# Hashed attention and top-1 experts on one core: block transpositions behind the first product, and six steps moved between pairs

## The chip, the core and the metric

One NeuronCore of a Trainium2 chip runs the whole program. The metric is device microseconds of one execution; a kernel's time is the median of its runs.

## What is computed

Bucketed attention over 4 batches of 8 heads, 768 tokens of 64 elements, then a mixture of 8 experts in which each of the 3072 tokens goes to one:

```python
q_bits = (np.einsum('bhsd,dk->bhsk', q, proj) > 0)      # 6 bits; k_bits the same way
mask = q_bucket[:, :, :, None] == k_bucket[:, :, None, :]
scores = np.where(mask, scale * np.matmul(q, k.transpose(0, 1, 3, 2)), -1e9)
attn = np.exp(scores - scores.max(-1)); attn /= attn.sum(-1) + 1e-09
x = np.matmul(attn, v)                                  # to (3072, 512)
expert_idx = np.argmax(x @ w_gate, axis=1)
for e in range(8):
    y[expert_idx == e] = np.maximum(x[expert_idx == e] @ w1[e], 0.0) @ w2[e]
return gate_w[:, None] * y
```

## The kernel before

**Attention part (0 to some 460 us).** Heads are worked off in 16 pairs (g = 0 to 15, four to a batch). A pair has twelve units of 128 query rows (six for each head). Unit i goes through S (score, four matrix products, L306 and L308), R (row maximum on VectorE, DVE, L316), A (its factor, L321 to L325, on DVE or GpSimd, POOL), X (exponential on ScalarE, ACT, L332), which frees the score's buffer in PSUM, of which there are three. The first six units are then transposed on TensorE (PE) (T, L346) and copied out (E, L370 or L372); the last six are transposed in blocks on DVE (D, L386), and the next pair sends them to `pt` with 16 transfers (L396): Y0, three of four block rows, twelve transfers, and Y1, the last four. V and B are the products with the values (L407), of which B10 is the first that uses exchanged `pt`. O, K, L and M bring the result to token rows `xr` (L412, L426, L436, L416).

For the next pair, G and H compute the hash bits (L261, L241), w scales them on ACT and writes them to DRAM (`lsh_bits`, L274 and L275), and z reads them into the operands as mask rows (`mask`, L279, on POOL's queue). C are POOL's casts and subtractions of the next pair's q and k (`part`, L205 to L213).

Once a batch (four pairs) is done, its tokens are routed in the second pair that follows (`route`, steps Z0 to Z6 in pairs 5, 9 and 13) and their rows are scattered to `sorted_rows`, six scatters a batch (`scatter`, steps N0 to N3, L498 to L501, on POOL). In a pair the N steps come in the order N2 (early), N0 (middle), N3 and N1 (end). `sorted_rows` is first filled with empty rows, eight fills, one an expert (`fill`, L147), issued from `before`.

The order of all this is written by hand: the strings HEAD, NEXT, PLAN and LAST list the steps of pair 0, 1, 2 to 14 and 15, and every engine, and the DMA queue of SyncE (SP), executes its share in this order. A "-" behind a step means the pair before.

From the first three batches' counts `pick_first` chooses the expert to begin with, in four pieces: the keys (L518 to L521), their maximum (L528, L530), the index (L534 to L536), and its load into SP's register (L539), after which the first raw weights are loaded.

**Expert part.** Nine phases of a first product (`mm1`, eight column groups f, L774), ReLU in two parts (`relu`: high on ACT, L788, low on DVE, L790) and a second product (`mm2`, L811, or by token in `yout`, L831). Phases 0 and 1 are 256 tokens each of the first expert, phases 2 to 8 one expert each, of 456 down to 354 tokens. While phase n runs, the rows of n+1 are read (`rows`, `xg`), transposed in blocks on DVE (`blocks`, L722, four or three of them), and split into high and low parts (`xt`: ACT L741, DVE L742). The raw weights of the next expert are split on ACT and POOL (`halves`, L679, L680). In phases 3 to 5 small steps of a plan for spilled tokens run on DVE between them (L572 to L635).

Of the kernel before, what the change touches and what calls it, by code (L numbers as in the profile page):

```python
# [53 lines left out]
def lsh_attention_moe(ctx, tc, qk2, v, proj, wg, w1, w1q, w2, out):  # L54
# [17 lines left out]
    def load_x(h):  # L72
        g = h // 2
        if g == NG - 1:
            x = (wk if h % 2 else moe).tile([128, 2 * S], F32, name="xl" if h % 2 else "xhe", bufs=1)
        else:
            x = room[:, h % 2] if g % 2 else wk.tile([128, 2 * S], F32, name="xd")
        for c in ((S, 2 * S), (0, S)) if h < 2 else ((0, 2 * S),):
            nc.sync.dma_start(x[:, c[0]:c[1]], qk2[h][:, c[0]:c[1]])
        XD[h] = x  # L80

    def load_v(g):
        VT[g] = wk.tile([128, NT, 2, D], F32, name="vt")
        nc.sync.dma_start(VT[g], v[g])
# [409 lines left out]
    def scatter(b, hf, ts=(0, 1, 2)):  # L494
        slot, x = SL[b, hf], XR[b, hf]
        t0 = b * NT + hf * 3
        if ts[0] == 0:
            nc.gpsimd.tensor_copy(x[:, :, GC + 1].bitcast(I32), C["tokid"][:, t0:t0 + 3])  # L498
        for t in ts:
            nc.gpsimd.memset(C["spacer"], 0.0)  # L500
            st = nc.gpsimd.indirect_dma_start(  # L501
                out=xs, out_offset=bass.IndirectOffsetOnAxis(ap=slot[:, t:t + 1], axis=0),
                in_=x[:, t], in_offset=None)
            for o in scat:
                tc.declare_no_dep(st.ins, o.ins, reason="slots of other tokens")
            scat.append(st)
# [9 lines left out]
    def keys(name):  # L516
        k = const.tile([128, E], F32, name=name)
        nc.vector.tensor_tensor(k, C["base"], C["base0"], op=OP.subtract)  # L518
        C["cnt"] = const.tile([128, E], F32, name=name + "_c")
        nc.vector.tensor_copy(C["cnt"], k)  # L520
        nc.vector.scalar_tensor_tensor(k, k, float(E), C["desc"], op0=OP.mult, op1=OP.add)  # L521
        return k

    def pick_first():
        k = keys("key0")
        yield
        t = const.tile([128, 4], F32, name="pf")
# [255 lines left out]
    M1 = {}  # L783
# [8 lines left out]
    def by_token(n):  # L792
        return PH[n][2] <= 384
# [87 lines left out]
        nc.sync.dma_start(wgt[:, :, s * (PW - E):s * (PW - E) + E], wg[:, :, s * E:(s + 1) * E])  # L881
    NC = NU // 2
    FREE = ("00v", "10v")
    routes, parts, pick = {}, list(range(16)), pick_first()

    def weights(n):
# [8 lines left out]
    def weight_half(op, x):  # L895
# [30 lines left out]

    NEXT = """
        S0 E40a- R0 L0- S1 X11- S2 T41- E41a- C00 C01 C02 A0V T42- E42a- X0 T50- E50a- T51- E51a- T52- E52v- G R1 A1P
        R2 S3 H A2V X1 R3 X2 V1- T00 C03 E00v A3P C04 S4 O1- M1- T01 S5 X3 R4 E01a C05 A4V R5 A5V T02 T10 w X4 E02a
        C06 E10v S6 R6 X5 A6V S7 C10 C11 T11 E11a T12 S8 E12v K1- L1- T20 X6 R7 T21 S9 E20a E21a A7P z0 R8 A8P C12 X7  # L930
        T22 R9 A9P X8 E22a D6 S10 D7 S11 C13 D8 X9 B00 R10 C14 z1 A10P R11 A11P B01 C15 D9 X10 X11 C16 D10 D11 M0 M1
    """.split()

    PLAN = """
        Y0- S0 R0 O0- S1 S2 C00 C01 C02 A0V X0 G R1 A1P R2 S3 H A2V X1 R3 K0- X2 L0- T00 C03 E00v A3P C04 S4 Z0 T01 S5
        X3 R4 E01a C05 A4V Z1 R5 A5V T02 T10 w Y1- X4 N2 E02a C06 E10v S6 R6 X5 A6V S7 Z2 C10 Z3 Z4 C11 T11 E11a Z5
        T12 S8 E12v T20 X6 R7 T21 S9 Z6 E20a N0 E21a A7P z0 R8 A8P C12 X7 T22 R9 A9P X8 E22a B10- D6 S10 D7 S11 C13 D8
        B11- X9 B00 R10 C14 z1 A10P R11 A11P B01 C15 D9 X10 X11 N3 O1- C16 K1- N1 D10 D11 M0 M1 L1-
    """.split()

    LAST = """
        Y0- S0 O0- R0 K0- S1 L0- X0 Y1- R1 S2 S3 R2 X1 X2 S4 T00 T01 R3 E00a E01a R4 S5 X3 R5 T02 X4 X5 E02v T10 S6
        E10a T11 T12 E11a R6 S7 T20 S8 R7 E12a T21 X6 S9 E20v X7 E21v B10- B11- O1- M0 R8 T22 E22a x0 R9 X8 T30 X9 g0
        V0 E30a x2 h0 O0 T31 S10 g2 E31a T40 T32 h2 R10 E40a S11 T41 R11 E32a K0 E41v nA m0 L0 r0 X10 T42 X11 nA E42a
        T50 M1 tP E50a r0 m1 T51 nA r0 T52 E51a m2 E52a tP tV u0 u1 nP r0 tP u2 r0 r0 nA V1 d0 nP r0 O1 tP d1 K1- K1
# [13 lines left out]
    def scatter_step(g, k):  # L959

        b, q = divmod(g - NP, NP)
        if 0 <= b < B - 1:
            at = {(q, k): 2 * q + k - 2 for q in (1, 2, 3) for k in (0, 1)}
            if b == B - 2:
                at |= {(2, 2): 2, (2, 0): 3, (2, 3): 4, (2, 1): 5}
            if (q, k) in at:
                scatter(b, at[q, k] // 3, (at[q, k] % 3,))

    def before(c):

        g, r = divmod(c, 6)
        if r == 3 and g + 2 < NG:
            load_x(2 * g + 4)
            load_x(2 * g + 5)
        if g + 1 < NG and r == (5 if g else 4):
            load_v(g + 1)
        if g < 2 and r > 3:
            fill(4 * g + 2 * r - 8)
            fill(4 * g + 2 * r - 7)

    def behind(i):

# [10 lines left out]
    def step(g, w):  # L993
# [7 lines left out]
        if op == "S":  # L1001
            i = 12 * n + int(x)
            if i % 2 == 0:
                before(i // 2)
# [26 lines left out]
        elif op == "E":  # L1031
            trans_ev(6 * n + int(x[0]), int(x[1]), x[2] == "v" and not (n % NP == 1 and n > NP and x in FREE))
        elif op == "V":
# [45 lines left out]
    last = [route(B - 1, (0,)), route(B - 1, (1,))]  # L1079
    for g in range(NG):  # L1080
        for w in {0: HEAD, 1: NEXT, NG - 1: LAST}.get(g, PLAN):
            step(g, w)
            if g == NG - 2 and w in ("R5", "R7", "R9", "S11"):
                next(pick, None)
                if w == "S11":
                    raw_load(0, 0)
                    raw_load(0, 1)
            if g == NG - 1 and w == "R9":
                GT[0] = moe.tile([128, 4], F32, name="gate", bufs=3)
                nc.vector.tensor_copy(GT[0][:, :2], XG[0][:, :, GC])  # L1090
                tokens(0)
# [18 lines left out]
    def halves(n, k):  # L1110

        if n < 4 * E:
            chunk_part(n + k // 4, k % 4)
            if k % 2:
                h = 2 * n + k // 2 + 3
                if h < LASTH:
                    raw_load(h // 2, h % 2)


    WHEN = (((0,), (1,)), ((2,), (3,)), ((), ()), ((), ()))  # L1120
    raw_load(5, 0)
    plan = spill_plan()
    for n in range(1, len(PH)):
        c0 = 4 * (PH[n][0] + 1)
        last = n + 1 == len(PH)
        if not last:
            rows(n + 1)
        for f in range(8):
            mm1(n, f)
            if f % 2 and not by_token(n - 1):  # L1130
                yout(n - 1, f // 2)
            halves(c0, f)
            if not last and f > 3:
                blocks(n + 1, f - 4)
            if 3 <= n < 6:
                for _ in range(2):
                    next(plan, None)
        for m in range(4):
            mid, end = ((), ()) if last else WHEN[m]
            if not (last and m == 3):  # L1140
                mm2(n, m, lambda: xts(n + 1, mid))
            halves(c0 + 2, 2 * m)
            halves(c0 + 2, 2 * m + 1)
            xts(n + 1, end)
        if n == 6:
# [69 lines left out]
```

## Time and profile before

| | |
|---|---|
| median of 3 runs | 763.74 us (760.83 to 765.19) |
| profiled execution | 767.85 us |
| its span, first to last instruction | 766.1 us |
| PE busy | 718.8 us, 94% |
| DVE, ACT, POOL busy | 489.8, 413.8, 487.2 us |
| mean granted clock of PE | 0.977 |

The times are those of one core, so the span is nearly the whole time. A busy PE is not a PE at its peak, since matrix products are pipelined, but an idle one is lost time. A wait in square brackets behind a row is the idle time of that engine just before it, with what is taken to have ended it; where an instruction waits for several things, only the last by the profile is named.

### The profile page before, as it was taken

To read this page: it belongs to the slowest core of one execution; us is meant where nothing else is said; L and a number is where in the kernel's file an instruction comes from. 1 tells how busy PE (TensorE), PEld (TensorE's weight loads), DVE (VectorE), ACT (ScalarE), POOL (GpSimd) and SP (SyncE) were. 2 spreads that over 40 slices of the span, in tenths; PEclk is the share of its full clock that TensorE was granted. 3 is DMA by queue.
4 is the path that set the end of the run, shared out by engine and by line. 5 is a ranking of instruction groups with operands and counts; after the bars stand their busy time and mean duration, and the time that the engine had idled before them with its cause. 6 is when DMAs were issued, how large, how long until landed. Compare 5 with 4: busy or idle time off the path is not lost.

```text
span 766.1 us, 13486 instructions
## 1 busy us (share of the span) xinstructions
PE 718.8 (94%) x4575; PEld 577.4 (75%) x4575; DVE 489.8 (64%) x936; ACT 413.8 (54%) x836; POOL 487.2 (64%) x729
## 2 busy tenths in 40 slices
PE   8997899999989999999988999699999999999996
PEld 3765676667757766676566788589989899989895
DVE  6757888889879888998797672324573825242321
ACT  5765766677658666776566632434334344453310
POOL 8635656677767687866766563384656666668532
PEclk7999999999999999999999999899999999999999
DMA  5949776768787768786649336664737386737301
GB/s 188 297 135 327 212 194 177 206 187 216 200 222 203 219 159 221 222 237 157 195 130 247 125 133 189 174 164 159 179 104 181 136 127 180 188 130 197 113 10 37
DMA packets 69928, 135.58 MB, mean 177 GB/s; under 512 B 15572, under 2 KB 32212, under 8 KB 69857
## 3 DMA queue, kind: packets, MB, share of 16 engines
q1 hardware_dynamic: 63024, 118.31, 56.4%
q0 software_dynamic: 6688, 16.35, 6.4%
q8 instruction: 37, 0.61, 0.4%
q14 instruction: 35, 0.28, 0.1%
q10 hardware_dynamic: 144, 0.03, 0.0%
HBM read 75.79 MB, written 26.33 MB: 133 GB/s over the span
## 4 chain that ended last, share of the span: by engine, by line
PE 65%; DVE 11%; issue 7%; ACT 7%; POOL 5%; DMA 4%; SPq 1%; POOLq 0%; DVEq 0%; ACTq 0%; another core or an unknown queue 0%
PE s L774 14%; PE t L407 14%; PE s L811 10%; PE s L831 8%; PE s L306 6%; DVE m L316 5%; ACT e L332 5%; PE s L308 5%; PE t L346 4%; PE t L426 2%; DMA xg<-sorted_rows 2%; ACT pt L372 1%; DMA pt<-w 1%; DMA qk<-masks 1%; POOL m L321 1%
## 5 line engine op out<-in xcount | busy, mean ns | idle before, releaser
L332 ACT ACTIVATE e<-s,m 128x768 f32<-128x768 f32 x192 | 189.9, 992 | 90.7 <-POOL m L325 45.0
L316 DVE TENSOR_REDUCE m<-s 128x1 f32<-128x768 f32 x192 | 178.2, 948 | 23.0 <-PE s L308 17.2
L680 POOL TENSOR_TENSOR w<-raw,w 128x512 fp32r<-128x512 f32 x112 | 144.8, 1320 | 45.4 <-ACT w L679 44.9
L407 PE MATMUL t<-pt,vt 128*64 128x384 f32 x768 | 131.7, 493 | 4.1 <-DMA pt<-w 2.2
L774 PE MATMUL s<-xh,w 128*128 128x456 f32 (+6 forms) x672 | 126.8, 346 | 0.0
L774 PEld LDWEIGHTS s<-xh,w 128*128 128x128 f32 x672 | 119.2, 188 | 3.0
L407 PEld LDWEIGHTS t<-pt,vt 128*64 128x64 f32 x768 | 52.7, 137 | 67.9 <-issue 64.4
L346 PE MATMUL t<-ident,e 128*128 128x128 f32 x648 | 94.5, 279 | 5.3 <-DVE pt L370 2.8
L790 DVE SCALAR_TENSOR_TENSOR hh<-s,hh 128x256 fp32r<-128x256 f32 (+7 forms) x64 | 35.3, 551 | 91.3 <-ACT hh L788 89.9
L386 DVE STREAM_TRANSPOSE w<-e 128x768 f32<-128x768 f32 x84 | 79.1, 963 | 15.7 <-ACT e L332 13.9
L346 PEld LDWEIGHTS t<-ident,e 128*128 128x128 f32 x648 | 77.1, 143 | 15.9 <-ACT pt L372 4.9
L788 ACT ACTIVATE hh<-s 128x256 fp32r<-128x256 f32 (+7 forms) x64 | 31.3, 489 | 100.3 <-PE s L774 100.3
L321 POOL TENSOR_SCALAR m<-m 128x1 f32<-128x1 f32 x98 | 22.8, 232 | 92.5 <-DVE m L316 89.3
L811 PE MATMUL s<-hh,w 128*128 128x456 f32 (+3 forms) x384 | 76.4, 360 | 3.6 <-DVE hh L790 3.6
L811 PEld LDWEIGHTS s<-hh,w 128*128 128x128 f32 x384 | 72.3, 191 | 7.0 <-DVE hh L790 4.1
L679 ACT ACTIVATE w<-raw 128x512 fp32r<-128x512 f32 x112 | 66.9, 623 | 11.1 <-DMA raw<-in_w1q_dram 8.5
L372 ACT ACTIVATE pt<-t 128x512 f32<-128x512 f32 (+1 forms) x119 | 67.3, 588 | 7.7 <-PE t L346 6.9
L844 POOL DMA_INDIRECT out_dram<-y,ix x26 | 26.7, 1027 | 67.9 <-DVE y L842 45.6
L306 PE MATMUL s<-w 80*128 80x384 f32 x192 | 57.0, 378 | 11.3 <-ACT e L332 10.8
L306 PE MATMUL s<-qk 80*128 80x384 f32 x192 | 58.3, 387 | 7.6 <-DMA qk<-masks 3.2
L831 PE MATMUL s<-w,hh 128*128 128x512 f32 (+1 forms) x240 | 58.8, 406 | 5.8 <-DVE hh L790 5.8
L831 PEld LDWEIGHTS s<-w,hh 128*128 128x128 f32 (+1 forms) x240 | 46.3, 194 | 17.1 <-DVE hh L790 6.0
(219 smaller groups left out, 1077.1 us busy)
## 6 DMA issues: line engine op xcount, KB each, us to landing
pt<-w SPq DMA_DIRECT2D x224, 144.0 KB, 3.3
raw<-in_w_dram SPq DMA_DIRECT2D x36, 512.0 KB, 4.3
raw<-in_w1q_dram SPq DMA_DIRECT2D x28, 512.0 KB, 3.6
w<-in_qk_dram SPq DMA_DIRECT2D x14, 768.0 KB, 7.8
xd<-in_qk_dram SPq DMA_DIRECT2D x14, 768.0 KB
sorted_rows<-xr SPq DMA_DIRECT2D x8, 1156.0 KB, 17.8
vt<-in_v_dram SPq DMA_DIRECT2D x16, 384.0 KB, 3.3
xg<-sorted_rows SPq DMA_DIRECT2D x16, 256.0 KB, 5.8
```

What stands on the lines that cost most here:

```text
L306: nc.tensor.matmul(p[:, a, :HALF], k[0:80, 2, c], k[0:80, 3, n], start=i >= 4, stop=i < 4)
L316: nc.vector.tensor_reduce(m[:, 0:1], p[:, :, :HALF], axis=AX.XY, op=OP.max, negate=True)
L332: nc.scalar.activation(e, p[:, :, :HALF], AF.Exp, bias=m[:, 2:3], scale=m[:, 1:2], accum_out=SM[g, hf][:, t, s:s + 1])
L346: nc.tensor.transpose(p[:, x * 128:(x + 1) * 128], e[w][:, kt // 3, (kt % 3) * 128:(kt % 3) * 128 + 128], ident)
L372: nc.scalar.activation(o, x, AF.Copy)
L386: nc.vector.transpose(d.rearrange("p b k q -> p k b q"), PP.pop(i).rearrange("p a c -> p (a c)"))
L407: nc.tensor.matmul(p[s * 64:(s + 1) * 64, :HALF], VT[g][:, kt, s, :], x, start=(kt == 0), stop=(kt == NT - 1))
L679: nc.scalar.activation(w[:, 0, a], r, AF.Copy)
L680: nc.gpsimd.tensor_tensor(w[:, 1, a], r, w[:, 0, a], op=OP.subtract)
L774: nc.tensor.matmul(p[:, :c], w[:, a, d, fs], x[:, b, d, :c], start=(k == 0), stop=(k == 11))
L811: nc.tensor.matmul(p[:, :c], w[:, a, f % 4, ms], h[b][:, f, :c], start=(k == 0), stop=(k == 23))
L831: nc.tensor.matmul(p[:pw], HH[n][b][:, f, i:i + pw], w[:, a, f % 4], start=(k == 0), stop=(k == 23))
```

## The change

Nothing is added or taken away in the computation; instructions move.

- **Block transpositions.** `blocks(n + 1, j)` for all j is issued ahead of phase n's second product instead of one each behind the first product's last four column groups. The token splits `xt` start half a block later; in phase 1 they all move into its second tile.
- **Empty rows.** All eight fills are issued in pair 0, four each at two places, instead of four in pair 0 and four in pair 1.
- **Bits.** w moves from behind T10 to behind X2, in NEXT and in PLAN, and takes Y1 along in PLAN. In LAST Y1 moves ahead of X0; no other transfer lies between.
- **Scatters.** The first of a batch moves from the middle (N0) to the end (N1) of the routing pair, and the others by one place; the last goes to the middle of the fourth pair behind. For batch 2 only the first moves, to N3 of pair 13.
- **Pick.** Its four pieces move from R5, R7, R9 and S11 of pair 14 to M1 of pair 13 and S3, X2 and S8 of pair 14; the loads of the first raw weights move with the last.

```diff
+    PICK = ((NG - 3, "M1"), (NG - 2, "S3"), (NG - 2, "X2"), (NG - 2, "S8"))
...
-        Y0- S0 R0 O0- S1 S2 C00 C01 C02 A0V X0 G R1 A1P R2 S3 H A2V X1 R3 K0- X2 L0- T00 C03 E00v A3P C04 S4 Z0 T01 S5
-        X3 R4 E01a C05 A4V Z1 R5 A5V T02 T10 w Y1- X4 N2 E02a C06 E10v S6 R6 X5 A6V S7 Z2 C10 Z3 Z4 C11 T11 E11a Z5
+        Y0- S0 R0 O0- S1 S2 C00 C01 C02 A0V X0 G R1 A1P R2 S3 H A2V X1 R3 K0- X2 w Y1- L0- T00 C03 E00v A3P C04 S4 Z0
+        T01 S5 X3 R4 E01a C05 A4V Z1 R5 A5V T02 T10 X4 N2 E02a C06 E10v S6 R6 X5 A6V S7 Z2 C10 Z3 Z4 C11 T11 E11a Z5
...
-        if 0 <= b < B - 1:
-            at = {(q, k): 2 * q + k - 2 for q in (1, 2, 3) for k in (0, 1)}
-            if b == B - 2:
-                at |= {(2, 2): 2, (2, 0): 3, (2, 3): 4, (2, 1): 5}
-            if (q, k) in at:
-                scatter(b, at[q, k] // 3, (at[q, k] % 3,))
+        for b, q in ((b, q), (b - 1, q + NP)):
+            if 0 <= b < B - 1:
+                t = (LATE if b == B - 2 else OFTEN).get((q, k))
+                if t is not None:
+                    scatter(b, t // 3, (t % 3,))
+
+    OFTEN = {(1, 1): 0, (2, 0): 1, (2, 1): 2, (3, 0): 3, (3, 1): 4, (4, 0): 5}
+    LATE = {(1, 3): 0, (1, 1): 1, (2, 2): 2, (2, 0): 3, (2, 3): 4, (2, 1): 5}
...
-        if g < 2 and r > 3:
-            fill(4 * g + 2 * r - 8)
-            fill(4 * g + 2 * r - 7)
+        if g == 0 and r > 3:
+            for e in range(4):
+                fill(4 * r - 16 + e)
...
-            if g == NG - 2 and w in ("R5", "R7", "R9", "S11"):
+            if (g, w) in PICK:
                 next(pick, None)
-                if w == "S11":
+                if w == PICK[-1][1]:
                     raw_load(0, 0)
                     raw_load(0, 1)
...
-    WHEN = (((0,), (1,)), ((2,), (3,)), ((), ()), ((), ()))
+    WHEN = (((), (0,)), ((1,), (2,)), ((3,), ()), ((), ()))
+    SOON = (((), ()), ((0, 1), (2, 3)), ((), ()), ((), ()))
...
             halves(c0, f)
-            if not last and f > 3:
-                blocks(n + 1, f - 4)
...
         for m in range(4):
-            mid, end = ((), ()) if last else WHEN[m]
+            mid, end = ((), ()) if last else (WHEN if n > 1 else SOON)[m]
+            if m == 0 and not last:
+                for j in range(4):
+                    blocks(n + 1, j)
```

SP's queue in pairs 0 to 2, before (`sorted_rows<-xr` are the fills, `masks<-bits` the bits' writes, `xd` and `w_69` loads of q and k, `vt` of values):

```order
L84 DMA vt<-in_v_dram 128x768
L147 DMA sorted_rows<-xr 512x1x578 x4
L275 DMA masks<-bits 128x384
L79 DMA w_69<-in_qk_dram 128x1536 x2
L147 DMA sorted_rows<-xr 512x1x578 x2
L84 DMA vt<-in_v_dram 128x768
L147 DMA sorted_rows<-xr 512x1x578 x2
L396 DMA pt<-w_743 32x1152 x12
```

and now:

```order
L84 DMA vt<-in_v_dram 128x768
L147 DMA sorted_rows<-xr 512x1x578 x8
L275 DMA masks<-bits 128x384
L79 DMA w_69<-in_qk_dram 128x1536 x2
L84 DMA vt<-in_v_dram 128x768
L396 DMA pt<-w_745 32x1152 x12
```

The last four fills now stand ahead of pair 2's bits and loads instead of behind them.

POOL in the middle of pair 5, before (L498 to L501 is the scatter, L321 and L325 a unit's factor, L279 a mask read):

```order
L207 CAST qk<-xd 128x768
L498 COPY xr<-tokid_i 128x3
L500 MEMSET spacer 1x1
L501 DMA sorted_rows<-xr,slot 25600x578
L321 TENSOR_SCALAR m<-m 128x1
L325 TENSOR_TENSOR m<-m 128x1
L279 DMA qk<-masks 16x4x384
```

and now:

```order
L207 CAST qk<-xd 128x768
L321 TENSOR_SCALAR m<-m 128x1
L325 TENSOR_TENSOR m<-m 128x1
L279 DMA qk<-masks 16x4x384
```

The scatter now stands behind the pair's last subtraction (L213).

DVE in phase 1, before (L790 is the low part of a ReLU, L722 a block transposition):

```order
L790 SCALAR_TENSOR_TENSOR hh_5707<-s,hh_5706 128x256 x5
L722 STREAM_TRANSPOSE xt<-xg 128x4x4x32
L790 SCALAR_TENSOR_TENSOR hh_5707<-s,hh_5706 128x256
L722 STREAM_TRANSPOSE xt<-xg 128x4x4x32
L790 SCALAR_TENSOR_TENSOR hh_5707<-s,hh_5706 128x256
L722 STREAM_TRANSPOSE xt<-xg 128x4x4x32
L790 SCALAR_TENSOR_TENSOR hh_5707<-s,hh_5706 128x256
L722 STREAM_TRANSPOSE xt<-xg 128x4x4x32
```

and now:

```order
L790 SCALAR_TENSOR_TENSOR hh_5707<-s,hh_5706 128x256 x8
L722 STREAM_TRANSPOSE xt<-xg 128x4x4x32 x4
L842 TENSOR_SCALAR y<-s,gate 128x512
L739 COPY gate<-xi 128x4
L711 COPY ix<-xi 128x4
L742 TENSOR_TENSOR xh<-xt,xh 128x456 x2
L842 TENSOR_SCALAR y<-s,gate 128x512
L742 TENSOR_TENSOR xh<-xt,xh 128x456 x2
```

All low parts now stand ahead of the transpositions, and the last two token splits behind the second tile's scaling (L842).

## Rows read from the trace of the kernel before

**Rows 1.** PE by pair (2, 4, 5, 6, 14): stretch, length, PE busy, clock, DMA, GB/s.
```profile
69.20:100.40 31.20, 27.17 (x178) 0.89 0.84 244
125.30:149.70 24.40, 23.77 (x178) 1.00 0.69 191
149.70:176.50 26.80, 24.71 (x185) 1.00 0.66 183
176.50:200.90 24.40, 23.78 (x178) 1.00 0.83 226
379.20:407.90 28.70, 25.83 (x179) 0.94 0.59 152
```
**Rows 2.** Fills, GB/s in 1-us slices from 40 us, mask reads, SP's `pt` issues.
```profile
L147 SPq DMA_DIRECT2D sorted_rows<-xr x8: 550/698/1222, 21.9 to 57.1; - x8
...
GB/s 349 324 242 46 0 0 0 0 8 0 0 0 0 101 181 295 369 332 221 302 396 421 280 342 216 156 303 370 391 399 398 365 326 340 326 353 286 270 240 240
...
L279 POOL DMA_DIRECT2D qk<-masks x14: 558/587/603, 59.5 to 372.8; - x14
...
68.32 12.55 SPq L396 DMA_DIRECT2D pt<-w  x12
```
**Rows 3.** Waits of PE, 60 to 100 us: total, times, longest.
```profile
PE s L306 <- DMA qk<-masks: 3.2, 2, 1.8
PE t L407 <- DMA pt<-w: 2.2, 1, 2.2
```
**Rows 4.** Timeline of pair 5 (start, us, what, idle before), and the waits.
```profile
163.74 1.13 POOL L501 DMA_INDIRECT sorted_rows<-xr,slot  x1 [2.27 <-issue]
...
165.50 0.99 ACT L332 ACTIVATE e<-s,m 128x768 f32<-128x768 f32 x1 [2.36 <-POOL m L325]
...
166.63 0.62 PE L306 MATMUL s<-w 80*128 80x384 f32 x2 [0.95 <-ACT e L332]
...
POOL sorted_rows L501 <- DVE xr L490: 4.3, 2, 2.2
```
**Rows 5.** Timeline of pair 7, PE.
```profile
215.79 2.16 PE L407 MATMUL t<-pt,vt 128*64 128x384 f32 x12 [1.88 <-ACT e L332]
```
**Rows 6.** Timeline of pair 4, ACT and DVE.
```profile
130.68 0.99 ACT L332 ACTIVATE e<-s,m 128x768 f32<-128x768 f32 x1 [0.22 <-POOL m L325]
...
132.14 0.61 ACT L274 ACTIVATE bits<-bits,wsg 64x384 f32<-64x384 f32 x1
132.64 0.98 ACT L332 ACTIVATE e<-s,m 128x768 f32<-128x768 f32 x1
...
132.19 0.21 DVE L323 TENSOR_SCALAR m<-m 128x1 f32<-128x1 f32 x1
```
**Rows 7.** Timeline of pair 14, DVE, POOL and PE.
```profile
387.05 1.76 DVE L518 TENSOR_TENSOR key<-pb,base 128x8 f32<-128x8 f32 x1
...
394.12 0.26 DVE L530 TENSOR_SCALAR first<-key,pf 128x8 f32<-128x8 f32 x1
...
387.76 1.02 POOL L213 TENSOR_TENSOR w<-xhe,w 64x384 fp32r<-64x384 f32 x1
...
391.31 0.66 PE L346 MATMUL t<-ident,e 128*128 128x128 f32 x4 [2.25 <-DVE pt L370]
```
**Rows 8.** Timeline of phase 1, DVE, PE and ACT, and PE's stretch.
```profile
485.29 0.71 DVE L722 STREAM_TRANSPOSE xt<-xg 128x512 f32<-128x512 f32 x1 [8.17 <-DMA xg<-sorted_rows]
...
486.36 13.68 PE L831 MATMUL s<-w,hh 128*128 128x512 f32 x48 [5.81 <-DVE hh L790]
...
486.56 0.63 ACT L679 ACTIVATE w<-raw 128x512 fp32r<-128x512 f32 x1 [5.82 <-DMA raw<-in_w1q_dram]
487.10 0.37 ACT L788 ACTIVATE hh<-s 128x256 fp32r<-128x256 f32 x1
...
484.50:491.40 6.90, 5.04 (x12) 0.51 0.62 211
```
**Rows 9.** PE's waits ahead of second products, and the stretch of phase 3's.
```profile
PE s L811 <- DVE hh L790: 3.6, 2, 1.8
...
560.00:583.00 23.00, 21.21 (x103) 0.93 0.34 102
```

More of the change, by code (lines that the diff above doesn't have):

```diff
@@ L928, in lsh_attention_moe @@
         S0 E40a- R0 L0- S1 X11- S2 T41- E41a- C00 C01 C02 A0V T42- E42a- X0 T50- E50a- T51- E51a- T52- E52v- G R1 A1P
-        R2 S3 H A2V X1 R3 X2 V1- T00 C03 E00v A3P C04 S4 O1- M1- T01 S5 X3 R4 E01a C05 A4V R5 A5V T02 T10 w X4 E02a
+        R2 S3 H A2V X1 R3 X2 w V1- T00 C03 E00v A3P C04 S4 O1- M1- T01 S5 X3 R4 E01a C05 A4V R5 A5V T02 T10 X4 E02a
         C06 E10v S6 R6 X5 A6V S7 C10 C11 T11 E11a T12 S8 E12v K1- L1- T20 X6 R7 T21 S9 E20a E21a A7P z0 R8 A8P C12 X7
@@ L941, in lsh_attention_moe @@
     LAST = """
-        Y0- S0 O0- R0 K0- S1 L0- X0 Y1- R1 S2 S3 R2 X1 X2 S4 T00 T01 R3 E00a E01a R4 S5 X3 R5 T02 X4 X5 E02v T10 S6
+        Y0- S0 O0- R0 K0- S1 Y1- X0 L0- R1 S2 S3 R2 X1 X2 S4 T00 T01 R3 E00a E01a R4 S5 X3 R5 T02 X4 X5 E02v T10 S6
         E10a T11 T12 E11a R6 S7 T20 S8 R7 E12a T21 X6 S9 E20v X7 E21v B10- B11- O1- M0 R8 T22 E22a x0 R9 X8 T30 X9 g0
```

## The prediction

> **What bounds the kernel now.** I read the stretches by pair first, then the waits of TensorE (PE), then, for each pair or phase that is long, the rows of the engines around its wait. A pair without trouble (pair 4) takes 24.4 us and PE is busy for 23.77 of them at full clock [rows 1]: PE is the bound, so time is lost only where PE stands still, or runs at the lower clock after it stood still. Such places are few, and each is longer than pair 4 by a known amount [rows 1]: pair 2 by 6.8, pair 5 by 2.4 (pairs 9 and 13 are its likes), pair 14 by 4.3. The expert part adds phases 1, 3 and 4. The change touches every one of these places, so its worth is a sum over them.
>
> **The empty rows (pairs 1 and 2).** Each fill writes 1.18 MB. Four go out in pair 0, from 21.9 us, four in pair 1, the last at 57.1 [rows 2]. Between 44 and 52 us the DMA engines move nothing; from 53 on they are full [rows 2]. So the masks' reads of pair 1 (from 59.5) and the twelve transfers of `pt`, whose issue stretches over 12.55 us from 68.32, share the engines with the late fills [rows 2]. PE then waits 3.2 us for masks and 2.2 for `pt` [rows 3], and the granted clock over pair 2 is 0.89 [rows 1], which is 31.2 x 0.11 = 3.4 us of full-speed work lost at the lower level (1.2 GHz). With all eight fills in pair 0, four more are 4.7 MB, at the 0.3 to 0.4 MB/us of the full stretches about 14 us: the idle gap takes them and they end near 57. Pair 2 should fall to about pair 4 (-6.8), and 1.4 of the 3.2 lies ahead of its start; I leave 0.7 for what is not clean: **-7.5**, between -3.5 (only `pt` and its share of the clock) and -8.2. Beside the sum: the Trainium skill (DMA: Bandwidth & Descriptors, "Queues, rings and completion order") says that descriptors of one ring are consumed in ring order on each DMA engine. By that the write of pair 2's bits, next on SP, lies behind all eight fills; that is the first rival. No row before shows eight in a row.
>
> **Scatters.** In pair 5 the scatter in mid-pair stands on POOL 2.27 us before it starts and then takes 1.13 [rows 4]; in the other two pairs of its kind the same wait, 4.3 in two, is put down to the reciprocal L490 of the routing [rows 4]. A7P, the factor of the next exponential, is behind it on POOL: ScalarE (ACT) waits 2.36 for it, then PE 0.95 for ACT [rows 4]. The change puts this scatter at the pair's end, when its slots are long known. Worth 1.1 in each of three pairs (PE's wait and a trifle behind it), **-3.4**; the bounds are 0.95 and the pair's whole 2.4, and I stay near PE's wait because the routing's own reductions and products stay. The added middle scatters of pairs 8 and 12 cost nothing: pair 6 has one in the middle and one at the end and takes 24.4 [rows 1]. Pair 13 gets two at its end, which pushes the next pair's casts on POOL by 1.4; POOL waits for a maximum there anyway, so nothing.
>
> **The last four `pt` transfers.** In pair 7 PE waits 1.88 ahead of the first product with exchanged `pt` [rows 5]. The row names ACT, but ACT was long done; the transfers come last there. They now go out with the bits, one exponential earlier, some 1.8 us: **-1.9**, between 0 and -1.9, since it is a matter of a landing.
>
> **The bits (w).** In pair 4 exponential X4 starts at 132.64, right behind the bits' scaling (132.14, 0.61 us), while its factor was ready at 132.40 [rows 6]. Without the scaling there X4 starts about 0.17 earlier, and the next score waits for it. In front of X3 (130.68, after an idle 0.22 [rows 6]) the 0.5 us it takes hide in part. Ten pairs without routing: **-1.7**, between +2.0 (X3 later by 0.2 in each) and -2.5.
>
> **The first expert's pick.** In pair 14 the first key operation, on 8 columns, takes 1.76 us, and PE then waits 2.25 for the copy behind it [rows 7]; the clock over the pair is 0.94 [rows 1]. The keys move to the end of pair 13, under PE's long run of value products, where VectorE (DVE) has under 2 us to spare; the other five small operations sit between maxima that the chain runs through, at up to 0.26 each [rows 7] about 0.9. I leave 0.4 for the keys: 4.3 - 1.3, **-3.0**, between -1.0 and -4.3. Next to it: GpSimd's subtraction L213 ran to 388.78 and the key ended at 388.81 [rows 7]. The Trainium skill (SBUF — State Buffer, "Who interferes with whom") says that a VectorE operation with two SBUF inputs contends with GpSimd, and that whoever comes second is blocked until the first is done; the rows agree. By that rule the keys would be blocked again, since POOL has casts and scatters back to back there: the second rival.
>
> **Block transpositions.** In phase 1 DVE stands 8.17 us for the next rows (`xg`) in front of its first transposition, with three of the relu parts behind it; PE waits 5.81 for them and starts the second product at 486.36; from 484.5 to 491.4 the granted clock is 0.51 [rows 8], 3.4 us lost. Behind the relus nothing of this is left, but ACT also waits, until 486.56, for a raw weight ahead of the last relu, which runs at 487.1 [rows 8]. PE would reach that relu's product after 21 of 24, at 480.55 + 21 x 0.214 ((13.68 - 3.4) / 48 each) = 485.05, and stand about 2.4. So 3.4 of the 5.81 are saved, and half of the lost clock, 1.7: **-5.1**, between -2.5 (the next expert's tokens late instead) and -9.2 (everything). In phases 3 and 4 PE waits 3.6 in two for a relu part [rows 9]; two of the four transpositions, 0.71 each [rows 8], stand ahead of it: 1.4 less in each. The clock of phase 3's second product is 0.93 over 23 us [rows 9], 1.6 lost, which goes with its wait: **-4.4**, between -1.4 and -5.2. In their new place the four (2.8 us) and the later token copies lie beside a second product of some 20 us, and PE wants their results only at its end: nothing.
>
> Sum: 7.5 + 3.4 + 1.9 + 1.7 + 3.0 + 5.1 + 4.4 = 27.0. The profiled execution took 767.85, so 740.9; the median of the runs, 763.74, is 4.1 lower, which would make 736.7. Stalls on a DMA's landing need not be as long in the unprofiled runs, so I stay near the first: **740**.
>
> **Rivals.**
> - *The fills crowd out pair 1.* If the bits written behind eight fills land late, POOL stands at its mask read at 59.5 and pair 2 starts late. The first term becomes nothing: 740 + 7.5 = 747.5. For it: the full stretch of 53 to 80 us shows how slow a crowd is. Against it: the idle gap. Chance 0.13.
> - *The keys wait for GpSimd again.* Three blocked operations of 0.7 to 1.8 us end 1.5 to 2 after DVE's spare time, straight on the chain: the third term falls by 2 and the kernel lands at 742 to 743. Chance 0.2. It is what the rule of the Trainium skill (SBUF — State Buffer) would do here.
> - *The stalls are mostly the profile's.* The profiled execution is 4.1 longer than the median; if that is all stalls on DMA, about half of the DMA terms (7.5, 1.9, 5.1) are not there to be gained: 747. Chance 0.1.
> - *The tokens come late in every phase (slower than before).* The copies now start half a column block later, behind the four transpositions. If the last subtraction ended after PE's last product of a phase, each of seven phases would wait for about the transpositions' 2.8 and then lose 1.7 to the lower clock: 7 x 4.5 = 31.5, in all 740 + 31.5 = 771.5. It decides where less than one block (about 5 us) is left between the last copy and the next first product; a second product has three or four blocks and the last copy sits in the third. Phase 1, with two, is the only close one. Chance 0.02.
>
> **How the numbers follow.** Forecast 0.52, rivals as above, no measurable gain for reasons I can't name 0.03. All but the last two cases are faster by more than 0.5% (3.8 us, about what a measurement can tell from no change): faster 0.95, same 0.03, slower 0.02. Terms seldom all miss to one side; all low ends together give some 754, all high ends 725. With the rivals at 747 inside, 731 to 750 holds eight in ten.
>
> **What would show it.** Right: pair 2 within 1 us of pair 4; pairs 5, 9 and 13 near 25.7 with no wait of the scatter; pair 14 under 26; PE starting phase 1's second product by 481 and standing 1 to 3 us for the last relu; no wait of PE on L790 in phases 3 and 4. Wrong: a wait of PE for `xh` at the start of phases 2 to 8, of POOL for the bits near 60 us, a key operation over 1 us at the end of pair 13 with the next maximum late, or pairs 3 and 4 longer than 24.5, which would say that the bits cost in front of X3.

## The result, and the profile after

The changed kernel takes **742.51 us** (median of 4 runs, 741.69 to 744.0) beside 763.01 for the kernel before: ratio 0.9734, 95% interval 0.97 to 0.9767. A later set of runs of the same program (below) gives **739.87** (6 runs, 737.84 to 740.69) beside 762.34, ratio 0.9695 (0.9668 to 0.9722). The forecast of 740 lies between the two. What separates their profiled executions (744.0 and 740.02) is the one step that went wrong in the first; the other three runs of the first set have no profile, so for them this is not shown.

First the page of the changed kernel, then its stretches by pair (pairs 1, 2, 4, 5, 7 and 14, from each pair's first maximum; these answer to [rows 1]) and phase 1's and phase 3's second product. The columns are the stretch, its length and the busy time of PE, PEld, DVE, ACT and POOL with their instructions, then granted clock, DMA share and GB/s.

```profile
PE 709.8 (96%) x4575; PEld 571.5 (77%) x4575; DVE 486.6 (66%) x936; ACT 412.8 (56%) x836; POOL 487.6 (66%) x729
```
```profile
39.00:75.50 36.50, 30.00 (x192) 19.93 (x191) 22.13 (x40) 20.57 (x41) 16.33 (x30) 0.91 0.83 247
75.50:99.90 24.40, 23.79 (x178) 17.34 (x177) 21.28 (x37) 17.27 (x35) 16.36 (x30) 1.00 0.74 202
124.70:149.10 24.40, 23.80 (x178) 17.35 (x178) 21.27 (x37) 17.26 (x35) 16.34 (x30) 1.00 0.71 194
149.10:174.60 25.50, 24.24 (x185) 17.41 (x184) 22.24 (x46) 18.31 (x38) 18.83 (x38) 1.00 0.66 187
198.90:223.20 24.30, 23.68 (x178) 17.22 (x177) 21.26 (x37) 17.27 (x35) 18.89 (x35) 1.00 0.81 220
371.90:397.10 25.20, 23.93 (x179) 17.20 (x178) 22.32 (x43) 17.49 (x35) 20.61 (x40) 1.00 0.77 208
...
472.00:479.00 7.00, 5.57 (x25) 4.12 (x24) 4.32 (x10) 3.96 (x8) 3.17 (x4) 1.00 0.47 168
541.70:561.00 19.30, 19.30 (x101) 18.47 (x100) 10.69 (x16) 7.46 (x16) 12.19 (x11) 1.00 0.37 119
```

Pairs 2, 5, 7 and 14 are all within 1.2 us of pair 4 now, and phase 3's second product runs without a gap at full clock ([rows 9] had 0.93). Pair 1 alone is long: 36.5 us, against 31.3 before, at a granted clock of 0.91. The timeline of the changed kernel shows why, and the other places after it (start, duration, engine, line, operation; in brackets the idle time before it):

```profile
22.81 24.02 SPq L147 DMA_DIRECT2D sorted_rows<-xr  x8
49.42 0.75 SPq L275 DMA_DIRECT2D masks<-bits  x1
...
64.27 0.58 POOL L279 DMA_DIRECT2D qk<-masks  x1 [3.70 <-DMA masks<-bits]
...
65.42 0.99 ACT L332 ACTIVATE e<-s,m 128x768 f32<-128x768 f32 x1 [3.73 <-POOL m L325]
...
66.56 1.01 PE L306 MATMUL s<-w 80*128 80x384 f32 x2 [3.84 <-ACT e L332]
...
164.00 0.99 ACT L332 ACTIVATE e<-s,m 128x768 f32<-128x768 f32 x1 [0.19 <-POOL m L325]
...
171.48 1.13 POOL L501 DMA_INDIRECT sorted_rows<-xr,slot  x1 [0.27 <-POOL xr L498]
...
204.60 0.35 SPq L275 DMA_DIRECT2D masks<-bits  x1
205.00 2.44 SPq L396 DMA_DIRECT2D pt<-w  x4
...
368.97 1.02 POOL L213 TENSOR_TENSOR qk<-xd,qk 64x384 fp32r<-64x384 f32 x1
...
369.54 0.48 DVE L518 TENSOR_TENSOR key<-pb,base 128x8 f32<-128x8 f32 x1
...
374.76 1.01 POOL L211 TENSOR_TENSOR w<-xhe,w 80x384 fp32r<-80x384 f32 x1
...
375.09 0.70 DVE L530 TENSOR_SCALAR first<-key,pf 128x8 f32<-128x8 f32 x1
...
473.74 0.63 ACT L679 ACTIVATE w<-raw 128x512 fp32r<-128x512 f32 x1 [6.01 <-DMA raw<-in_w1q_dram]
```

The eight fills leave SP from 22.8 on and are still moving when pair 2's bits are issued at 49.42. GpSimd stands 3.70 us for these bits, then ScalarE for the factor behind it, then PE 3.84 for ScalarE; behind this wait the granted clock is 0.51, the 1.2 GHz level:

```profile
66.00:73.00 7.00, 6.45 (x20) 3.09 (x22) 5.48 (x7) 4.02 (x9) 6.42 (x13) 0.51 0.16 41
```

In pair 5 the mid-pair scatter is gone and ScalarE waits 0.19 instead of the 2.36 of [rows 4]; in pair 7 the bits leave 5.7 us into the pair, the last four `pt` transfers right behind them, and PE has no wait for `pt` [rows 5]; the first key operation, now at the end of pair 13, takes 0.48 instead of 1.76 [rows 7]. In phases 1 to 8 PE stands for one thing only, the last relu of phase 1 (1.43 us), behind ScalarE's 6.01 for a raw weight.

### The profile page after: what moved, and what is told of

The parts are those of the page before. It is cut to its first block, busy times and chain, and to the rows that moved or that the text cites. A ratio compares the mean times of both kernels' runs of the same rounds, so it can differ in the third digit from the quotient of the medians.

```text
span 742.2 us, 13477 instructions
## 1 busy us (share of the span) xinstructions
PE 709.8 (96%) x4575; PEld 571.5 (77%) x4575; DVE 486.6 (66%) x936; ACT 412.8 (56%) x836; POOL 487.6 (66%) x729
## 4 chain that ended last, share of the span: by engine, by line
PE 73%; ACT 8%; DVE 6%; issue 5%; DMA 3%; POOL 2%; SPq 1%; ACTq 0%; POOLq 0%; another core or an unknown queue 0%; DVEq 0%
PE t L407 17%; PE s L774 16%; PE s L811 10%; PE s L306 7%; PE s L831 7%; PE t L346 6%; PE s L308 6%; ACT e L332 5%; DVE m L316 4%; PE t L426 2%; DMA masks<-bits 2%; ACT pt L372 1%; DMA raw<-in_w1q_dram 1%; PE s L840 1%; ACT bits L241 1%
## 5 line engine op out<-in xcount | busy, mean ns | idle before, releaser
L407 PE MATMUL t<-pt,vt 128*64 128x384 f32 x768 | 133.2, 497 | 0.0
L790 DVE SCALAR_TENSOR_TENSOR hh<-s,hh 128x256 fp32r<-128x256 f32 (+7 forms) x64 | 35.5, 555 | 105.4 <-ACT hh L788 104.0
L346 PEld LDWEIGHTS t<-ident,e 128*128 128x128 f32 x648 | 75.5, 141 | 17.5 <-ACT pt L372 8.0
L788 ACT ACTIVATE hh<-s 128x256 fp32r<-128x256 f32 (+7 forms) x64 | 31.3, 490 | 92.5 <-PE s L774 92.5
L321 POOL TENSOR_SCALAR m<-m 128x1 f32<-128x1 f32 x98 | 22.8, 232 | 84.7 <-DVE m L316 82.4
L811 PE MATMUL s<-hh,w 128*128 128x456 f32 (+3 forms) x384 | 74.9, 355 | 0.0
L831 PE MATMUL s<-w,hh 128*128 128x512 f32 (+1 forms) x240 | 56.7, 395 | 1.4 <-ACT hh L788 1.4
L831 PEld LDWEIGHTS s<-w,hh 128*128 128x128 f32 (+1 forms) x240 | 44.5, 187 | 12.4 <-ACT hh L788 1.9
## 6 DMA issues: line engine op xcount, KB each, us to landing
w<-in_qk_dram SPq DMA_DIRECT2D x14, 768.0 KB, 4.9
xd<-in_qk_dram SPq DMA_DIRECT2D x14, 768.0 KB, 6.3
```

The source lines that it names most:

```text
L346: nc.tensor.transpose(p[:, x * 128:(x + 1) * 128], e[w][:, kt // 3, (kt % 3) * 128:(kt % 3) * 128 + 128], ident)
L407: nc.tensor.matmul(p[s * 64:(s + 1) * 64, :HALF], VT[g][:, kt, s, :], x, start=(kt == 0), stop=(kt == NT - 1))
L811: nc.tensor.matmul(p[:, :c], w[:, a, f % 4, ms], h[b][:, f, :c], start=(k == 0), stop=(k == 23))
L831: nc.tensor.matmul(p[:pw], HH[n][b][:, f, i:i + pw], w[:, a, f % 4], start=(k == 0), stop=(k == 23))
```

## Experiments

Whole times carry some 3 us of chance, about as much as pair 0 differs between profiles (last section), so the verdicts rest on the lengths of pairs and phases in the profiles (one profile a kernel), and the whole times only support them. "The change's" lengths are: pairs 1 and 2 36.50 and 24.37 in the first profile (31.02 and 25.44 in the repeat), pairs 5, 9, 13 25.44 to 25.70, pair 7 24.31, pair 14 25.23.

**e1: the fills back to four and four** (in `before`; w, scatters, pick and blocks as changed):

```diff
-        if g == 0 and r > 3:
-            for e in range(4):
-                fill(4 * r - 16 + e)
+        if g < 2 and r > 3:
+            fill(4 * g + 2 * r - 8)
+            fill(4 * g + 2 * r - 7)
```

> The change with the fills as before, four in pair 0 and four in pair 1, all else kept. Theory (in the change, pair 2's bits stand on SP behind eight fills: their write takes 14.56 us to land, POOL stands 3.7 us for it, pair 1 is 5.2 us longer, and this gives back what pair 2 gained): the bits' write lands within 7 us, pair 1 falls from 36.5 to 31.3 +- 0.7, pair 2 rises from 24.4 to 29 to 31, and the whole is 741 to 745, so the move of the empty rows by itself is worth nothing. Rival (pair 1 is longer because w now stands ahead of X3 and T00, not because of the fills): pair 1 stays above 34 and the whole is 746 to 750.

739.36 us (739.06 to 743.15), ratio 0.9692 (0.9644 to 0.9741). Pair 1 took 30.79, pair 2 27.09. The waits of PE in pairs 1 and 2 of this kernel have one line for masks, and none for `pt`:

```profile
PE s L306 <- DMA qk<-masks: 2.6, 1, 2.6
```

So with the late fills still there 4.1 of pair 2's 6.8 us are gone, more than the 0.2 to 2.2 expected: since w moved, the bits leave at 48.2, and the late fills start to issue at 49.6 and 51.7, where the last of them left at 57.1 before [rows 2]. The forecast had put the whole of it down to the fills.

**e2: pair 2's bits from ScalarE's queue**, where no fill stands ahead of them:

```diff
-        nc.sync.dma_start(md[g], r)
+        (nc.scalar if g == 2 else nc.sync).dma_start(md[g], r)
```

> The change, but pair 2's bits are written from ACT's queue instead of SP's, so that they don't stand behind the fills. Theory (what costs is the place in SP's queue): the write lands within 7 us instead of 14.56, POOL doesn't stand at its first mask read of pair 1, pair 1 is 31.3 to 32.5, pair 2 stays at 24.4, the whole is 737 to 739. Rival (the DMA engines are full until 72 us, whatever the queue): the write still takes over 10 us or the mask reads land late, pair 1 stays above 34.5, the whole 741 to 743.

736.07 us (734.99 to 740.19), ratio 0.9644 (0.9592 to 0.9697); pairs 1 and 2 30.80 and 25.19. GpSimd asks at once:

```profile
47.71 0.34 ACTq L275 DMA_DIRECT2D masks<-bits  x1
...
58.87 0.58 POOL L279 DMA_DIRECT2D qk<-masks  x1
```

The trace's packets say it more sharply than the times. The table has the start of the first and of the last of the bits' 128 packets (1536 bytes), and the end of the last fill packet (2312 bytes):

| kernel | queue | issued | bits' packets | fills end |
|---|---|---|---|---|
| before (four late fills, behind the bits) | SP | 52.87 | 53.7 to 54.3 | 77.3 |
| the change, first profile | SP | 49.42 | 57.4 to 63.5 | 63.0 |
| the change, repeat | SP | 49.30 | 55.1 to 59.9 | 59.4 |
| this kernel | ACT | 47.71 | 51.6 to 53.7 | 57.8 |

On SP's queue the bits come out with the tail of the fills; on ACT's they pass them, while the same fills are in flight. In all seven profiles with the bits behind eight fills on SP (the change twice, e3 to e7) the last bits' packet starts 0.4 to 0.5 us after the fills' end; in the two with the bits on ACT's queue (this kernel and e10) it starts 4.1 and 4.9 before it. The Trainium skill (DMA: Bandwidth & Descriptors, "Queues, rings and completion order") says that on each DMA engine the descriptors of one ring are consumed in order; the trace agrees.

**e8: five fills in pair 0, one in each of pairs 1, 2 and 3:**

```diff
-            for e in range(4):
-                fill(4 * r - 16 + e)
+            for e in ((0, 1, 2), (3, 4))[r - 4]:
+                fill(e)
+        if 0 < g < 4 and r == 4:
+            fill(4 + g)
```

> The change, but five fills in pair 0 and one each in the middle of pairs 1, 2 and 3. Theory (the fills cost only where a write or read that someone waits for shares the queue with several of them): pair 1 31.3 to 32, pairs 2 and 3 within 0.5 of 24.4 and 24.9, the whole 736.5 to 738.5. Rival (every fill in a pair costs some of the mask reads' or pt's landing, 1.2 to 2 us each): pairs 2 and 3 at 26 each, the whole 740 to 742.

737.83 us (736.7 to 739.6), ratio 0.9652 (0.9609 to 0.9695); pairs 1, 2 and 3 30.81, 25.08 and 24.89. Pair 3 is as long with a fill in it as in the repeat without one (24.89 and 24.87), so late fills did no harm here where they were few and stood behind the bits.

**e6: w and Y1 back behind T10** (in NEXT and PLAN; fills as changed):

```diff
-        ... A2V X1 R3 K0- X2 w Y1- L0- T00 ... T02 T10 X4 N2 ...
+        ... A2V X1 R3 K0- X2 L0- T00 ... T02 T10 w Y1- X4 N2 ...
```

> The change with w (and Y1 with it) back behind T10 in NEXT and PLAN. Theory (w behind X2 takes the scaling off the way to X4, worth 0.1 a pair, and Y1 earlier takes away pair 7's 1.9): ten pairs longer by 0.05 to 0.15, pair 7 at 24.4 to 26.3, pair 1 longer by up to 3 since the bits stand later still behind the fills; the whole 744 to 749. Rival (pair 7's wait came from elsewhere, and w costs in front of X3 what it gives at X4): the pairs within 0.03 and the whole within 1 of the change.

743.24 us (739.85 to 746.48), ratio 0.9722 (0.9665 to 0.9779). Pair 7 took 28.84, pair 14 26.21, the ordinary pairs 24.42 to 24.46 (0.1 more each), pairs 1 and 2 31.61 and 25.34. In pair 7 the bits leave 7.5 us into the pair, PE stands for the transfers behind them, and the granted clock over the pair is 0.94 (it was 1.00 before, with the shorter wait of [rows 5]):

```profile
199.11 0.33 SPq L275 DMA_DIRECT2D masks<-bits  x1
199.49 3.60 SPq L396 DMA_DIRECT2D pt<-w  x4
...
207.44 2.96 PE L407 MATMUL t<-pt,vt 128*64 128x384 f32 x12 [2.76 <-DMA pt<-w]
```

At the end of pair 1 GpSimd waited only 0.85 us for bits that were issued at 50.6, later than with the change: they left with the tail of the fills either way (57.3, the fills' end 56.9). Another execution of this kernel could lose more there; there is one profile.

**e7: Y1 alone back behind T10** (in PLAN), w as changed:

> The bits' scaling (w) stays early in a pair, the issue Y1 behind it goes back behind T10. Theory (pair 7 was saved by Y1, ordinary pairs by w): pair 7 takes 26.3 to 28.8 us again with PE standing about 2 ahead of the first product with exchanged rows, ordinary pairs stay at 24.3 to 24.35; the whole is 2 to 4 longer than the change's unless pair 1 is shorter. Rival (w itself did it): pair 7 at 24.3 and ordinary pairs at 24.4.

739.46 us (738.51 to 740.41), ratio 0.9681 (0.9649 to 0.9714). Pair 7 24.36, ordinary pairs 24.32 to 24.36. The expectation named the wrong step, and its rival holds: SP does the same as with the change,

```profile
200.22 0.33 SPq L275 DMA_DIRECT2D masks<-bits  x1
200.59 2.43 SPq L396 DMA_DIRECT2D pt<-w  x4
```

5.7 us into the pair. Nothing stands between the two places on SP's queue; what SP waits for is ScalarE's scaling. Before, SP issued them later in the pair, 7.4 us into it:

```profile
208.34 0.33 SPq L275 DMA_DIRECT2D masks<-bits  x1
208.72 3.81 SPq L396 DMA_DIRECT2D pt<-w  x4
```

The early w let pair 7's transfers go, Y1's own place did nothing there.

**e3: the scatters back:**

```diff
-        for b, q in ((b, q), (b - 1, q + NP)):
-            if 0 <= b < B - 1:
-                t = (LATE if b == B - 2 else OFTEN).get((q, k))
-                if t is not None:
-                    scatter(b, t // 3, (t % 3,))
+        if 0 <= b < B - 1:
+            at = {(q, k): 2 * q + k - 2 for q in (1, 2, 3) for k in (0, 1)}
+            if b == B - 2:
+                at |= {(2, 2): 2, (2, 0): 3, (2, 3): 4, (2, 1): 5}
+            if (q, k) in at:
+                scatter(b, at[q, k] // 3, (at[q, k] % 3,))
```

> The rows' scatters go back to their places before the change; all else is the change. Theory (a scatter in mid-pair holds A7P on GpSimd): pairs 5, 9 and 13 take 1.3 to 1.4 us more each than with the change (25.4 to 26.8), with GpSimd standing ahead of a scatter or of A7P by some 2 us again and PE by about 1; the whole is 4 longer than the change's 742.5, some 746. Rival (these pairs became shorter by w and Y1, or by the clock): they stay within 0.4 of 25.4 and the whole stays at 742 to 743.

744.13 us (742.79 to 746.32), ratio 0.9751 (0.9716 to 0.9785). Pairs 5, 9 and 13 took 26.95, 27.48 and 27.65, together 5.5 more than in the repeat, and more than the 3.9 to 4.2 that moving them had given (why is not shown); the chain of [rows 4] is back in pair 5, scatter, factor, exponential, score:

```profile
157.33 1.13 POOL L501 DMA_INDIRECT sorted_rows<-xr,slot  x1 [2.42 <-issue]
...
159.09 0.99 ACT L332 ACTIVATE e<-s,m 128x768 f32<-128x768 f32 x1 [2.35 <-POOL m L325]
...
160.22 0.62 PE L306 MATMUL s<-w 80*128 80x384 f32 x2 [0.94 <-ACT e L332]
```

**e4: the pick back in pair 14:**

```diff
-    PICK = ((NG - 3, "M1"), (NG - 2, "S3"), (NG - 2, "X2"), (NG - 2, "S8"))
+    PICK = ((NG - 2, "R5"), (NG - 2, "R7"), (NG - 2, "R9"), (NG - 2, "S11"))
```

> The first expert's pick goes back to its four places in pair 14; all else is the change. Theory (the pick's key operations and sums delay the maxima of pair 14): pair 14 takes some 28.7 us instead of 25.2, with the first key operation at 1 to 2 us again and PE standing about 2 behind it; the whole is 3.5 longer than the change's, some 746. Rival (pair 14 was long for the weights and the scatters around it): under 26.5 and the whole under 744.

741.55 us (739.27 to 744.63), ratio 0.9721 (0.9684 to 0.9758). Pair 14 took 28.39, as the theory says; the whole is too wide to tell 3 us, and is not used. Each of the three key operations ends with an operation of GpSimd (L213 at 374.03, L205 at 374.79, L207 at 375.57):

```profile
372.32 1.75 DVE L518 TENSOR_TENSOR key<-pb,base 128x8 f32<-128x8 f32 x1
374.10 0.73 DVE L520 COPY key_c<-key 128x8 f32<-128x8 f32 x1
374.87 0.73 DVE L521 SCALAR_TENSOR_TENSOR key<-key,desc 128x8 f32<-128x8 f32 x1
...
373.01 1.02 POOL L213 TENSOR_TENSOR w<-xhe,w 64x384 fp32r<-64x384 f32 x1
373.97 0.82 POOL L205 CAST w<-xl 128x768 fp32r<-128x768 f32 x1
374.75 0.82 POOL L207 CAST w<-xl 128x768 fp32r<-128x768 f32 x1
...
376.56 1.12 PE L346 MATMUL t<-ident,e 128*128 128x128 f32 x4 [2.38 <-DVE pt L370]
```

**e5: the block transpositions back into the first products**, token copies at their old steps:

```diff
+    OLD = (((0,), (1,)), ((2,), (3,)), ((), ()), ((), ()))
...
             halves(c0, f)
+            if not last and f > 3:
+                blocks(n + 1, f - 4)
...
-            mid, end = ((), ()) if last else (WHEN if n > 1 else SOON)[m]
-            if m == 0 and not last:
-                for j in range(4):
-                    blocks(n + 1, j)
+            mid, end = ((), ()) if last else (OLD)[m]
```

> The block transpositions go back into the first product of every phase, the token copies to their old steps; all else is the change. Theory (all that phases 1, 3 and 4 gained is from this part): phase 1 is 6 to 7 us longer with PE standing 5 to 6 ahead of its second product, phases 3 and 4 by 3.6 and 2.0; the whole is 11 to 12 longer than the change's, some 754. Rival (part of it is from the weights' order or the pick's earlier gather): under 5 in the whole.

748.63 us (745.86 to 752.88), ratio 0.9788 (0.9746 to 0.983). PE's waits in phases 1, 3 and 4 are back:

```profile
471.04 13.71 PE L831 MATMUL s<-w,hh 128*128 128x512 f32 x48 [5.24 <-DVE hh L790]
...
546.97 20.70 PE L811 MATMUL s<-hh,w 128*128 128x432 f32 x96 [1.80 <-DVE hh L790]
...
589.21 18.09 PE L811 MATMUL s<-hh,w 128*128 128x408 f32 x96 [1.81 <-DVE hh L790]
```

From the end of their first products to the next phase these three take 18.8, 22.8 and 20.2 us here, and 11.7, 19.2 and 18.2 in the repeat of the change: 12.7 in all. The profiled execution is 12.9 longer than that of the repeat; the median is only 8.8 longer, for the four executions lie 7 us apart and the profiled one is the longest of them. Which stage makes the others shorter no profile shows.

**a1: the change once more**, nothing edited ("the repeat"):

> The change once more, nothing edited. In its first profile pair 1 took 36.5 us behind the fills; in four later kernels with the same code in pairs 0 and 1 it took 30.7 to 31.3 and pair 2 25.2 to 25.8. Theory (GpSimd's first mask read waits for the bits in some executions only, as fast as the fills drain just then): here pair 1 is 30.7 to 31.3, the bits are there within 0.5 us of GpSimd's asking, and the median is 737 to 739. Rival (this kernel does it always, by where its buffers or code lie): pair 1 again 35 or more, the median again 742 to 743.

739.87 us, as told above; the median is 0.9 over the expected range. Pairs 1 and 2 of this kernel, then SP's and GpSimd's timeline, and PE in phase 1:

```profile
39.20:70.20 31.00, 27.92 (x196) 19.39 (x195) 21.92 (x41) 20.17 (x41) 15.51 (x29) 1.00 0.83 268
70.20:95.70 25.50, 22.91 (x173) 16.78 (x173) 21.53 (x38) 17.27 (x35) 17.30 (x32) 1.00 0.78 209
```
```profile
22.49 21.34 SPq L147 DMA_DIRECT2D sorted_rows<-xr  x8
49.30 0.34 SPq L275 DMA_DIRECT2D masks<-bits  x1
...
60.70 0.58 POOL L279 DMA_DIRECT2D qk<-masks  x1 [0.25 <-DMA masks<-bits]
...
470.48 6.53 PE L831 MATMUL s<-w,hh 128*128 128x512 f32 x27 [0.47 <-ACT hh L788]
```

The bits come 0.25 us after GpSimd asks for them, and in four other kernels with the same code in pairs 0 and 1 (e3, e4, e5, e7) they came 0.49 late or in time. The place is a race with no margin, lost by 3.7 us in the first profile. The expectation that the wait comes in some executions only is borne out as far as this: of six profiles with this code in pairs 0 and 1 one shows a wait over 0.5 us.

**e9 and e10: the last relu of phase 1 ahead of the raw weights' last halves**, once on the spread fills of e8 and once on ScalarE's write of e2:

```diff
-            halves(c0, f)
+            if n > 1 or f < 6:
+                halves(c0, f)
...
+        if n == 1:
+            halves(c0, 6)
+            halves(c0, 7)
```

> Five fills in pair 0, one in each of pairs 1 to 3, and in phase 1 the raw weights' last halves are cast behind the last relu. Theory (TensorE's wait in phase 1 is for a relu behind ScalarE's wait for a raw weight): no such wait in any execution, phase 1's second product 11.3 us; where the wait did not show before, nothing is gained; 736 to 738. Rival (the casts come too late for phase 2): TensorE waits for weights in phase 2, 739 or more.

> All eight fills in pair 0 as in the change, pair 2's bits written from ScalarE's queue, and the last halves in phase 1 cast behind the last relu. Theory: no wait for the bits and none for the relu in any execution; 735 to 737 and never over 741, so faster than the change by what its slower executions lose (4 to 6 us) and by 1 to 2 at the median if those are rare. Rival: the write in ScalarE's queue delays an exponential of pair 1, pair 1 over 31.5, no gain.

737.41 us (736.42 to 739.02; ratio 0.9675, 0.9647 to 0.9704) and 736.73 (735.0 to 739.55; ratio 0.9672, 0.9642 to 0.9701). In both, phase 1's second product takes 11.3 us without a wait; in e9's timeline ScalarE still stands 4.66 for the raw weight, with no relu behind it:

```profile
462.24 11.29 PE L831 MATMUL s<-w,hh 128*128 128x512 f32 x48
...
467.49 1.16 ACT L679 ACTIVATE w<-raw 128x512 fp32r<-128x512 f32 x2 [4.66 <-DMA raw<-in_w1q_dram]
```

Both medians lie under the repeat's in the same set of runs, by 2.5 and 3.1, but the intervals overlap, and in e10's profile 3.3 of 5.0 us are pair 0's chance. What the profiles show of e10's two edits is the removal of two waits: some 1.2 us against the repeat (0.5 in pairs 1 and 2, 0.7 in phase 1) and some 6.6 against the first profile (4.9 and 1.7).

## Why the prediction was right, and where it was not

Profile against profile (767.85 before; 744.0 after, 740.02 in the repeat), by the steps of the sum:

| step | forecast | first profile | repeat |
|---|---|---|---|
| empty rows (pairs 1 and 2) | -7.5 | -1.6 | -6.0 |
| scatters (5, 9, 13) | -3.4 | -4.2 | -3.9 |
| last four `pt` (pair 7) | -1.9 | -2.1 | -2.0 |
| bits, ordinary pairs (3, 4, 6, 8, 10, 11, 12; the forecast is for ten pairs) | -1.7 | -0.6 | -0.5 |
| pick (pair 14) | -3.0 | -3.5 | -3.1 |
| phase 1 | -5.1 | -6.7 | -7.6 |
| phases 3 and 4 | -4.4 | -5.6 | -5.6 |
| pair 0 | 0 | +1.3 | +1.6 |
| the rest | 0 | -0.9 | -0.7 |
| sum | -27.0 | -23.9 | -27.8 |

- **Empty rows: the step that failed.** "... the idle gap takes them and they end near 57": the fills ended at 63.0 and 59.4, and the bits, next on SP, left with them, at 63.5 and 59.9, where GpSimd asked for them at 60.6 and 60.5. The sum had no wait for the bits (0.7 was left for "what is not clean"); it stood only as the first rival, at a chance of 0.13, and the first profile is nearly that rival to the letter: pair 2 fell by the 6.8 forecast, pair 1 rose by 5.2. The drain was sized too short: all of the 0.3 to 0.4 MB/us was given to the fills, but of 13.97 MB moved from 20 to 66 us in the first profile 9.5 were fills, the rest the pairs' own loads. From their first packet to their last the fills took 34.1 us there and 29.3 to 31.2 in the eight other profiles that have all of them in pair 0, where the forecast comes to some 29 (28.0, the first fill packet before, to 57). So the repeat is the common case, and what the forecast lacked there is any room behind the fills: the same race came out 0.25 late, and the term is -6.0.
- **Its cause was named too narrowly.** Pairs 1 and 2 together take 62.5 before, 57.9 with the early w alone (e1), 57.0 with the early fills alone (e6), 56.5 with both in the repeat, and 60.9 with both in the first profile. Either edit frees pair 2 of most of its loss; with one profile of each, the second adds 0.5 to 1.4, and all eight fills ahead of the bits bring the race.
- **Scatters, pick:** shown by putting each back (+5.5 in three pairs, +2.8 in one, against the repeat). Both rest on POOL: the scatter held A7P, and each key operation ended within 0.05 us of one of GpSimd's (e4). Coming second does not tell all of it: in [rows 7] the key began at 387.05, ahead of L213 (387.76), and still ended with it; GpSimd's scatter, from 386.63, ran when it began. What held it between the two is not shown. Of the second rival the mechanism is there (L518 now ends at 370.02, L213 on POOL at 369.99; L530 takes 0.70 instead of the 0.26 of [rows 7] and ends with L211), but it makes them only some 0.3 and 0.4 us longer. At the end of pair 13 this costs little: in e3 the keys' second and third operations took 0.77 and 0.73, and pair 13 was 0.2 longer than pair 9. For L530, between two maxima of pair 14, it is not shown to be free: PE still stands 0.61 us in pair 14 for the copy L436 behind the pick's operations.
- **Last four `pt`:** right in size, wrong in the step: w did it, not Y1 (e7).
- **Bits:** mis-sized. Putting w back costs 0.08 in an ordinary pair, the mean of the seven, not 0.17. The sign "pairs 3 and 4 longer than 24.5" does not tell for pair 3, which took 24.87 before and 24.88 after.
- **Phases:** mis-sized to the safe side. The wait for the last relu was forecast at 2.4 with half of the lost clock staying; it is 0 to 1.43 over the profiles, and in the first profile and the repeat no stretch at the lower clock is left in the phases (1.00 from 472 to 479). The token copies came in time (the fourth rival: PE stands 0.15 us for `xh` in the repeat and 0.26 in e9).
- **"The stalls are mostly the profile's":** not borne out. The repeat's profiled 740.02 and its median 739.87 agree, and of the other kernels some profiled executions lie above their median (e5) and some below (e4). Executions of the kernel before spread from 759.4 to 768.0 over all sets, so its profiled 767.85 was one of the longest. The sum was worked out from that one execution: by the medians of the same sets the change is worth 20.5 and 22.5 us, less than the 27.0 of the sum and the 23.7 from 763.74 to 740.
- **Luck.** That the repeat's -27.8 is so near -27.0 is so in part by chance of the terms: empty rows, bits and pair 0 gave 4.3 less than forecast, scatters, pick, `pt`, the phases and the rest 5.1 more. Pair 0's +1.3 and +1.6 go with the clock of those executions (last section) and were not in the forecast.

## What to carry to other kernels

A transfer that something waits for must not stand behind bulk writes on its queue: list what each queue holds ahead of it, in bytes, and when these are done, before bulk is moved into an "idle" stretch. Where two edits aim at one stall, price each alone, since either may take it and the second bring only a new risk. And where a transfer's landing and its use lie within 1 us, one profile shows one outcome; look at several kernels that share the code.

## What was not expected of the hardware

- **Pair 0 has no fixed length, and it goes with the clock.** Of thirteen profiles four show 27.3 to 28.4 us and nine 29.1 to 31.0, though most have the same code there. The rows are 4 to 24 us of e10 (pair 0 27.4 us), e2 (28.4), before (29.1) and the repeat (30.6); the granted clock is the third number from the end, and PE's lower level is 1.2 GHz:

```profile
4.00:24.00 20.00, 16.45 (x109) 10.79 (x108) 15.57 (x32) 14.62 (x31) 17.03 (x21) 0.91 0.68 229
4.00:24.00 20.00, 16.94 (x101) 10.62 (x99) 14.11 (x29) 13.21 (x27) 16.66 (x20) 0.83 0.64 223
4.00:24.00 20.00, 17.49 (x97) 10.07 (x95) 13.71 (x28) 12.45 (x25) 15.19 (x18) 0.74 0.54 194
4.00:24.00 20.00, 17.36 (x91) 10.19 (x89) 12.79 (x24) 11.74 (x24) 14.67 (x18) 0.66 0.53 185
```

  Twelve profiles line up: 0.91 with 27.3 to 27.4 us (e4, e6, e10), 0.83 with 28.4 (e2), 0.74 with 29.1 (before, e1, e3, e9), 0.66 with 30.4 to 30.6 (first profile, repeat, e5, e7). In the thirteenth, e8 (31.0), the trace has no clock record ahead of 24.1 us, so the 1.00 that its row gives there is no reading. This is about the 3 us of chance in the whole times. Why an execution stays at the lower level longer is open.
- **The same transfers, slower.** From 50 to 60 us the DMA engines were as busy in the first profile as in the repeat (share 1.05) and moved 283 GB/s against 307; 339 against 367 from 30 to 40. A median fill packet took 0.107 us against 0.100, and 0.099 to 0.100 in the seven other profiles with all fills in pair 0. The fills' first packet started at 28.9 and 28.7 and their last ended 3.6 apart, which is what turned 0.25 us of delay into 3.7; where the lower rate came from is open.
